# A scheduler priority of 450 instructions for four steps of each slot in a chunked attention kernel

## The chip, the cores and the metric

The kernel runs on one core of one Trainium2 chip. The metric is the device time of one execution in microseconds (us). A core has five engines that each work through their own queue in order: TensorE (PE in the rows, its weight loads PEld), VectorE (DVE), ScalarE (ACT), GpSimd (POOL), and SyncE (SP), which here only issues DMA transfers. They meet through semaphores.

## What is computed

Three layers follow each other: a recurrent attention over 768 steps for 4 batches of 8 heads with 40 dimensions, a layer of 8 experts of which each token uses one, and a dense layer. The part that matters here is the first:

```python
state = np.zeros((B, H, D, D), dtype=np.float32)
for t in range(S):
    y[:, :, t] = np.einsum('bhd,bhde->bhe', rt, state)
    Sa = np.einsum('bhde,bhe->bhd', state, at)
    state_decay = state * wt[:, :, None, :] - np.einsum('bhd,bhe->bhde', Sa, bt)
    state = state_decay + np.einsum('bhd,bhe->bhde', vt, kt)
```

Then `x = _moe_ref(attention output)` and `_moe2_ref(x)`: 3072 tokens of 320 numbers through 1024-wide expert layers and a 2048-wide dense layer.

## The kernel before

The attention works in chunks of 64 steps. Two batches (bb 0 and 1) are taken side by side, and one **slot** is one chunk of one batch with its 8 heads: 12 chunks, 2 batches and 2 pairs of batches give 48 slots, and slots n and n + 2 are the same batch one chunk on. Eight slots (256 steps of two batches) form a **group**; there are six.

Each slot has a **chain** that carries the state from chunk to chunk:

- `stage_a` (L636): eight matmuls `sa` from `vg` and `pw`; ScalarE copies one half of the result into `va`, VectorE multiplies the other half with a mask into `va`.
- `stage_c` (L647): eight matmul pairs `yc` from `va` and `kbr`; VectorE adds the state `sm` and scales it back into `sm`.
- `stage_e` (L663): two transposes `tp` of `sm`, four ScalarE copies into `bds`.
- `stage_r` (L617): ScalarE copies `sm` into `vg`, matmuls `rp` from `bds`, ScalarE copies of `rp` into `vg` and `rs`. With `pw` this `vg` feeds `sa` two slots later.

Beside them stand steps that do not carry the state: `stage_p` (matmuls `pp` from `tt` and `la`, copied into `pw`), `stage_v` (matmuls `rvp`, copied into `vg`, masked by GpSimd into `va`), `stage_d` (output rows `rs`, `yt`) and the router (`xp`, `lg` and small VectorE work).

The rest is **filler**, work for later groups that is written down between the steps of the slots. `prepare` (L429) loads `wz`, `kb` and `ra` and makes two VectorE scans `s` and `q` for a later group; `products` and `sides` make matmuls `lp`, `bp`, `ap` in two PSUM banks, which ScalarE and VectorE empty into `l`, `kbr` and `la`. `inverse` (L516) makes the triangular inverses `tt` of the next group: a VectorE transpose `ul`, 31 pairs `tmp` and `ut` on VectorE, two VectorE transposes `ttc` and `t11`, GpSimd copies into `tt`, then for each half of the group matmuls `zp`, a ScalarE copy `z`, matmuls `yp` and ScalarE copies into `tt`. The `pp` of the next group's first slot needs this `tt`, so the first slot of a group (8, 16, 24, 32, 40) waits for the inverse of its group: the **boundaries** below.

During slot 40 the first expert's weights are loaded (`raw`) and split by ScalarE and VectorE into `we`, six pieces through three buffers. After slot 47 come the experts and the dense layer.

What sets the order: a scheduler takes all instructions of the program and fills each engine's queue. Among those that are ready by its own reckoning it takes the one that was written down first. `run` writes each slot in this order: `stage_a(n)`, `stage_e(n-1)`, filler, `stage_v`, `stage_p` and `stage_r` of slot n+1, `stage_c(n)`, filler, `stage_d(n-1)`, router, loads, filler. The queues are fixed once they are built; at run time each engine takes its next instruction alone and waits for it.

Of the kernel before, what the change touches and what calls it, by code (L numbers as in the profile page):

```python
# [283 lines left out]
class Attention:  # L284
# [330 lines left out]
                                pattern=[[0, 8], [1, C]], compare_op=ALU.is_gt, fill=0.0, base=0, channel_multiplier=-1)  # L615

    def stage_r(self, x):  # L617

        nc = self.nc
        if x.first and x.o.bp:  # L620
            nc.gpsimd.memset(self.sm[:, x.p2], 0.0)
            nc.gpsimd.memset(self.bds[:, x.p4], 0.0)
        for q in range(2):
            nc.scalar.copy(self.by2(x.vg[C:PP, :, q, :D]), self.halves(self.sm[q * HQ:q * HQ + D, x.p2]))
        rp = self.work("rp", [PP, 4, C])
        for i, u in x.prs:
            for r, c in ((slice(0, HQ), slice(0, HQ)), (slice(HQ, P), slice(HQ, PP))):
                nc.tensor.matmul(rp[c, i], lhsT=self.bds[r, u, :c.stop - c.start], rhs=x.r[r, u], start=True, stop=True)  # L628
        for q in range(2):
            nc.scalar.copy(x.vg[C:PP, :, q, D:], rp[q * HQ:q * HQ + D])  # L630
        x.rs = self.p.tile([PP, 4, C], F32, name="rs", bufs=3)
        nc.scalar.copy(x.rs, rp)

    def stage_a(self, x):

        nc = self.nc  # L636
        sa = self.work("sa", [P, 4, VG])
        for i, u in x.prs:
            for q in range(2):
                nc.tensor.matmul(sa[q * 64:q * 64 + 64, i], lhsT=x.pw[:, i, q * C:(q + 1) * C], rhs=x.vg[:, i, q, :], start=True, stop=True)  # L640
        for q in range(2):
            nc.scalar.copy(x.va[C:, :, q, :D], sa[q * 64:q * 64 + 64, :, :D])
        for q in range(2):
            r = slice(q * 64, q * 64 + 64)
            nc.vector.tensor_tensor(x.va[C:, :, q, D:], sa[r, :, D:], self.posmask[r].unsqueeze(1).to_broadcast([C, 4, C]), op=ALU.mult)

    def stage_c(self, x, s0_next):  # L647

        nc = self.nc
        kbr = x.o.kbr[x.half]  # L650
# [10 lines left out]
            nc.vector.tensor_tensor(sm, total, self.by2(s0_next[:, x.p4]).to_broadcast([PP, 2, 2, D]), op=ALU.mult)  # L661

    def stage_e(self, x):  # L663
        nc, k = self.nc, self.k
        tp = self.work("tp", [PP, 2, PP])
        for i in range(2):
# [657 lines left out]
```

## Time and profile before

| | |
|---|---|
| median of 3 runs | 1153.29 us (1152.75 to 1153.3) |
| profiled execution | 1149.13 us, of which the span of the instructions is 1147.3 us |
| slot 0 to slot 47 (first `sa` of each) | 87.3 to 514.1 us |
| experts and dense layer | from about 515 us to the end |
| PE, PEld, DVE, ACT, POOL busy in the span | 89%, 78%, 62%, 50%, 48% |
| PE, DVE, ACT busy between 87.3 and 514.1 us | 379, 322, 322 of 427 us |

Slots are counted by the first `sa` matmul of each. A matmul's record has a modelled end, so a busy PE need not be at its peak; idle time of an engine that nobody waits for costs nothing. In the rows, an arrow names what ended the idle time before an instruction.

### The profile page before, as it was taken

The page shows a single profiled execution, that of the slowest core. Times are in us where ns is not written, and L with a number is a line of the kernel's source. Part 1 is how long each engine was busy: PE and PEld are TensorE (multiplying, and loading weights), DVE is VectorE, ACT ScalarE, POOL GpSimd, SP SyncE. Part 2 cuts the span into 40 slices and gives each one's busy share as a digit, 9 for nine tenths or more (in the row PEclk, how much of TensorE's full clock was granted, in tenths as well). Part 3 has the DMA queues.
Part 4 walks back from the last instruction along what each step waited for, and adds up shares of the span by engine and source line. Part 5 has one row for each costly group of instructions (what it writes and reads, how often), then busy time and mean ns, then how long its engine had stood idle before and what let it go on. Part 6 is the DMA issues. An engine that isn't in the chain of part 4 may idle for free.

```text
span 1147.3 us, 24800 instructions
## 1 busy us (share of the span) xinstructions
PE 1016.7 (89%) x9597; PEld 895.2 (78%) x9597; DVE 715.6 (62%) x1469; ACT 568.4 (50%) x1426; POOL 548.5 (48%) x496
## 2 busy tenths in 40 slices
PE   2649788989899889798898889999999999999997
PEld 2538677867687777687787779999998999999996
DVE  8865887878959869444599984324444545354542
ACT  3637577867787878783554444442222212121211
POOL 6717367555675724233655535452434343434332
PEclk7659899988999999799999989999999999999999
DMA  4613223322322213525688775431000000000000
GB/s 118 203 52 96 63 56 91 89 69 69 94 85 69 56 41 76 137 60 172 179 279 256 242 236 168 131 116 38 24 24 23 23 24 24 23 23 19 29 1 26
DMA packets 98080, 103.35 MB, mean 90 GB/s; under 512 B 58404, under 2 KB 78884, under 8 KB 97956
## 3 DMA queue, kind: packets, MB, share of 16 engines
q1 hardware_dynamic: 95652, 93.83, 28.5%
q0 software_dynamic: 2304, 7.87, 2.1%
q8 instruction: 78, 1.28, 0.5%
q14 instruction: 46, 0.38, 0.1%
HBM read 79.39 MB, written 22.28 MB: 89 GB/s over the span
## 4 chain that ended last, share of the span: by engine, by line
PE 57%; DVE 22%; ACT 6%; issue 5%; DMA 5%; POOL 3%; SPq 0%; DVEq 0%; ACTq 0%; POOLq 0%
PE ph L238 20%; PE po L238 19%; DVE tmp L529 3%; PE lp L483 3%; PE pp L600 2%; DVE ut L531 2%; PE sa L640 2%; PE yc L656 2%; DMA raw<-in_moe_w_dram 2%; DVE s L455 2%; DVE dec L215 2%; DVE dec L218 1%; PE rp L628 1%; DVE q L457 1%; DVE dec L214 1%
## 5 line engine op out<-in xcount | busy, mean ns | idle before, releaser
L229 POOL TENSOR_TENSOR gl<-g,gh 128x512 fp32r<-128x512 f32 x96 | 123.9, 1293 | 211.2 <-ACT gh L228 127.1
L228 ACT ACTIVATE gh<-g 128x512 fp32r<-128x512 f32 x96 | 60.7, 632 | 249.4 <-DVE g L1214 174.5
L1213 DVE TENSOR_SCALAR g<-ph,al 128x512 f32<-128x512 f32 x96 | 72.1, 751 | 156.9 <-POOL gl L229 79.1
L238 PE MATMUL ph<-x2thi,win 128*128 128x512 f32 x480 | 157.0, 392 | 0.0
L238 PE MATMUL po<-wout,gh 128*128 128x320 f32 x768 | 139.1, 309 | 0.0
L238 PEld LDWEIGHTS po<-wout,gh 128*128 128x128 f32 x768 | 122.0, 188 | 5.4
L238 PE MATMUL ph<-x2tlo,win 128*128 128x512 f32 x288 | 113.5, 394 | 0.0
L238 PE MATMUL po<-we,hh 128*128 128x320 f32 (+1 forms) x480 | 91.5, 319 | 19.1 <-DVE hh L1089 13.4
L238 PE MATMUL ph<-xthi,we 128*128 128x448 f32 (+2 forms) x360 | 98.2, 344 | 2.8 <-DVE hl L1089 2.1
L238 PEld LDWEIGHTS ph<-x2thi,win 128*128 128x128 f32 x480 | 88.5, 188 | 13.2
L238 PEld LDWEIGHTS po<-we,hh 128*128 128x128 f32 (+1 forms) x480 | 74.5, 183 | 24.7 <-DVE hh L1089 14.8
L529 DVE TENSOR_TENSOR tmp<-ul,ut 128x31 f32<-128x31 f32 (+15 forms) x186 | 81.4, 437 | 3.7
L238 PE MATMUL po<-wout,gl 128*128 128x320 f32 x384 | 82.9, 311 | 0.0
L614 POOL TENSOR_SCALAR_AFFINE_SELECT va<-vg 64x512 f32<-64x512 f32 x48 | 35.2, 734 | 85.2 <-ACT vg L613 55.8
L238 PE MATMUL ph<-xtlo,we 128*128 128x448 f32 (+2 forms) x216 | 74.1, 344 | 0.3 <-DVE xtlo L271 0.3
L238 PEld LDWEIGHTS ph<-xthi,we 128*128 128x128 f32 x360 | 67.0, 196 | 7.0 <-issue 2.5
L464 POOL TENSOR_TENSOR abd<-ra,q 40x512 f32<-40x512 f32 x44 | 62.4, 1418 | 18.9 <-DVE q L457 5.3
L483 PE MATMUL lp<-kb,abd 128*128 128x128 f32 x352 | 56.4, 307 | 16.7 <-DMA wz<-in_wP_dram 10.7
L1214 DVE SCALAR_TENSOR_TENSOR g<-ph,g 128x512 f32<-128x512 f32 x96 | 66.3, 691 | 3.1
L656 PE MATMUL yc<-va,kbr 128*40 128x104 f32 (+3 forms) x768 | 57.2, 265 | 11.8 <-issue 8.5
L600 PE MATMUL pp<-tt,la 128*104 128x128 f32 x384 | 61.4, 309 | 6.1 <-DVE lg L902 4.1
L677 POOL TENSOR_TENSOR yt<-rs,q 104x256 f32<-104x256 f32 x46 | 34.4, 748 | 67.6 <-DVE rs L676 54.5
(212 smaller groups left out, 2358.0 us busy)
## 6 DMA issues: line engine op xcount, KB each, us to landing
raw<-in_moe_w_dram SPq DMA_DIRECT2D x16, 512.0 KB
rv<-in_rvP_dram SPq DMA_DIRECT2D x48, 160.0 KB
raw<-in_moe_w_dram SPq DMA_DIRECT2D x16, 480.0 KB
kb<-in_kbP_dram SPq DMA_DIRECT2D x44, 160.0 KB
r<-in_moe_w_in_dram SPq DMA_DIRECT2D x10, 512.0 KB
r<-in_moe_w_out_dram SPq DMA_DIRECT2D x10, 512.0 KB
xs_d<-tt SPq DMA_DIRECT2D x8, 560.0 KB
raw<-in_moe_w_dram SPq DMA_DIRECT2D x16, 256.0 KB
```

The lines of the kernel that those rows point to most:

```text
L228: nc.scalar.activation(hi, src, AF.Copy)
L229: return lo_eng.tensor_tensor(lo, src, f32(hi), op=ALU.subtract)
L238: return nc.tensor.matmul(out, lhsT=lhsT, rhs=rhs, start=start, stop=stop)
L464: nc.gpsimd.tensor_tensor(abd[r, :, q * C:(q + 1) * C], ra[r], qc[r, :, :C], op=ALU.mult)
L483: nc.tensor.matmul(lp[:, i], lhsT=abd[:, i, c2, :], rhs=kb[:, i, c2, :], start=True, stop=True)
L529: nc.vector.tensor_tensor(tv, ul[:, j, j + 1:].unsqueeze(2).to_broadcast([P, n, m]), ut[:, j, :m].unsqueeze(1).to_broadcast([P, n, m]), op ...
L600: nc.tensor.matmul(pp[:, i], lhsT=o.la[x.half][:, x.c2, u, :], rhs=o.tt[x.half][:, x.c2, u, :], start=True, stop=True)
L614: nc.gpsimd.affine_select(x.va[:C].rearrange("p a b c -> p (a b) c")[:, :, D:], x.vg[:C].rearrange("p a b c -> p (a b) c")[:, :, D:], patt ...
L656: nc.tensor.matmul(x.yc[r, i, a:], lhsT=kb[:, c], rhs=x.va[:, i, q, a:], start=True, stop=True)
L677: eng.tensor_tensor(yt[:PP, :, x.c2 * C:x.c2 * C + C], x.rs, x.o.q[x.half][:, x.p4, x.c2, :C], op=ALU.mult)
L1213: nc.vector.tensor_scalar(g, ph, 0.0, al[:, f:f + 1], op0=ALU.min, op1=ALU.mult)
L1214: nc.vector.scalar_tensor_tensor(g, ph, 0.0, g, op0=ALU.max, op1=ALU.add)
```

## The change

The bodies of `stage_r`, `stage_a`, `stage_c` and `stage_e` move into `do_r`, `do_a`, `do_c` and `do_e`, and the old names call these inside `high_priority(450)`: to the scheduler their instructions count as if they had been written down 450 instructions earlier. No instruction is added or taken away, `stage_p`, `stage_v`, `stage_d`, the router, the filler and all loads keep their place in the order of writing, and what each instruction depends on is the same.

```diff
     def stage_r(self, x):
+        with self.tc.high_priority(450):
+            self.do_r(x)
+
+    def do_r(self, x):
...
     def stage_a(self, x):
+        with self.tc.high_priority(450):
+            self.do_a(x)
+
+    def do_a(self, x):
...
     def stage_c(self, x, s0_next):
+        with self.tc.high_priority(450):
+            self.do_c(x, s0_next)
+
+    def do_c(self, x, s0_next):
...
     def stage_e(self, x):
+        with self.tc.high_priority(450):
+            self.do_e(x)
+
+    def do_e(self, x):
```

The lines below the first edit shift by 4, 8, 12 and 16; the names stay. The queues up to slot 0, and those of the experts and the dense layer from their first matmuls on, hold the same instructions in nearly the same order.

VectorE around the `va` of slot 8, before (`s`, `q`, `d1q` and `la` are filler, `ul` begins the inverse for slot 16):

```order
L455 SCALAR_TENSOR_TENSOR s<-wz_106,d1s_116 104x520
L491 TENSOR_TENSOR la<-lp,negmask_133 128x4x64
L457 SCALAR_TENSOR_TENSOR q<-wz_105,d1q_119 104x520
L456 RECIPROCAL d1q_119<-s 104x8
L457 SCALAR_TENSOR_TENSOR q<-wz_106,d1q_119 104x520
L645 TENSOR_TENSOR va_402<-sa,posmask_135 64x4x64 x2
L455 SCALAR_TENSOR_TENSOR s<-wz_105,d1s_116 104x520
L491 TENSOR_TENSOR la<-lp,negmask_133 128x4x64
L456 RECIPROCAL d1q_119<-s 104x8
L902 TENSOR_REDUCE lg<-xp 128x8
L522 STREAM_TRANSPOSE ul<-l_1632 128x1024
```

The same place on VectorE now (`va` of slot 8 is L653):

```order
L457 SCALAR_TENSOR_TENSOR q<-wz_106,d1q_119 104x520
L491 TENSOR_TENSOR la<-lp,negmask_133 128x4x64
L455 SCALAR_TENSOR_TENSOR s<-wz_105,d1s_116 104x520
L456 RECIPROCAL d1q_119<-s 104x8
L522 STREAM_TRANSPOSE ul<-l_1632 128x1024
L455 SCALAR_TENSOR_TENSOR s<-wz_106,d1s_116 104x520
L653 TENSOR_TENSOR va_402<-sa,posmask_135 64x4x64 x2
L529 TENSOR_TENSOR tmp<-ul,ut 128x31
```

A `la`, an `s`, the `ul` and a second `s` have moved from behind this `va` to ahead of it.

TensorE at the boundary to slot 40, before and, below, now (`yp` here is the second half of the group's inverse, with buffer numbers):

```order
L557 MATMUL zp_5802<-tt2_126,l1_4975 32x32 x32
L600 MATMUL pp_6259<-tt1_125,la_4977 104x128 x4
...
L565 MATMUL yp_5838<-z1_5835,t11_5719 32x32 x32
L640 MATMUL sa_6297<-vg1_406,pw0_416 64x104 x8
L667 MATMUL tp_6310<-ident_60,sm0_413 104x104 x2
```

```order
L557 MATMUL zp_5802<-tt2_126,l1_4975 32x32 x32
L600 MATMUL pp_6259<-tt1_125,la_4977 104x128
...
L600 MATMUL pp_6259<-tt1_125,la_4977 104x128 x3
L565 MATMUL yp_5838<-z1_5835,t11_5719 32x32 x23
L648 MATMUL sa_6297<-vg1_406,pw0_416 64x104
L683 MATMUL tp_6310<-ident_60,sm0_413 104x104
```

Where the dots stand come the eight `rp` of slot 40: now three of four `pp` follow them, and 9 of the 32 `yp` come behind `sa`.

ScalarE between the last two copies `xr` of slot 40 and the `rp` copies for slot 42, before and now (`we` from `raw_6860` and `raw_6864` are the fifth and sixth weight pieces, `va1` belongs to slot 41, `pw0` to slot 42):

```order
L1039 ACTIVATE we0_6647<-raw_6860 128x960
L901 COPY xr_6363<-xp_6365 128x320
L1039 ACTIVATE we0_6647<-raw_6864 128x640
L901 COPY xr_6364<-xp_6372 128x320
L642 COPY va1_403<-sa_6386 64x4x40 x2
L671 COPY bds0_411<-tp_6399 40x2x40 x4
L613 COPY vg0_404<-rvp_6406 64x4x64 x2
L602 COPY pw0_416<-pp_6418 104x512
```

```order
L917 COPY xr_6364<-xp_6372 128x320
L687 COPY bds0_411<-tp_6399 40x2x40 x4
L1055 ACTIVATE we0_6647<-raw_6860 128x960
L650 COPY va1_403<-sa_6386 64x4x40 x2
L613 COPY vg0_404<-rvp_6406 64x4x64 x2
L1055 ACTIVATE we0_6647<-raw_6864 128x640
L602 COPY pw0_416<-pp_6418 104x512
```

The sixth piece stood ahead of `va` of slot 41 and now stands behind it.

## Rows read from the trace of the kernel before

**Rows 1.** Page, part 1: busy us, share of the span, instructions.

```profile
PE 1016.7 (89%) x9597; PEld 895.2 (78%) x9597; DVE 715.6 (62%) x1469; ACT 568.4 (50%) x1426; POOL 548.5 (48%) x496
```

**Rows 2.** Windows: six groups of slots, the dense layer; columns stand in the first line.

```profile
core 0: us, PE busy (x) PEld busy (x) DVE busy (x) ACT busy (x) POOL busy (x), PEclk, DMA share, GB/s
87.27:179.92 92.65, 81.47 (x1225) 68.22 (x1225) 67.81 (x148) 64.19 (x200) 55.02 (x59) 0.94 0.29 76
179.92:260.79 80.87, 72.30 (x1039) 59.85 (x1039) 63.54 (x159) 59.84 (x190) 49.84 (x53) 0.92 0.31 79
260.79:336.24 75.45, 67.33 (x1020) 56.72 (x1016) 61.59 (x151) 57.73 (x176) 46.91 (x54) 0.91 0.29 77
336.24:411.88 75.64, 67.87 (x1021) 57.41 (x1020) 60.53 (x153) 57.06 (x176) 46.26 (x50) 0.93 0.26 67
411.88:467.61 55.73, 50.35 (x925) 41.91 (x923) 44.73 (x135) 44.62 (x130) 20.00 (x28) 0.97 0.35 88
467.61:514.07 46.46, 40.06 (x565) 33.37 (x561) 23.87 (x70) 38.50 (x107) 12.41 (x17) 0.89 0.31 76
...
770.00:1147.00 377.00, 369.44 (x2118) 335.85 (x2116) 164.19 (x246) 83.61 (x143) 149.62 (x122) 1.00 0.08 23
```

**Rows 3.** Windows, the same columns: slots 7 to 9, around the boundary to slot 8.

```profile
165.00:190.00 25.00, 24.88 (x424) 21.13 (x422) 13.83 (x26) 20.98 (x65) 21.37 (x24) 0.95 0.27 75
```

**Rows 4.** Timeline of VectorE at slot 8: start, us, instruction, shapes, [idle before].

```profile
185.83 0.88 DVE L645 TENSOR_TENSOR va<-sa,posmask 64x256 f32<-64x256 f32 x2
186.74 1.24 DVE L455 TENSOR_TENSOR_SCAN s<-wz,d1s 104x520 f32<-104x520 f32 x1
188.01 0.42 DVE L491 TENSOR_TENSOR la<-lp,negmask 128x256 f32<-128x256 f32 x1
...
189.73 2.00 DVE L522 STREAM_TRANSPOSE ul<-l 128x1024 f32<-128x1024 f32 x1 [0.96 <-POOL l L490]
```

**Rows 5.** Timeline of VectorE: where the inverse begins in two later groups.

```profile
263.34 1.91 DVE L522 STREAM_TRANSPOSE ul<-l 128x1024 f32<-128x1024 f32 x1
...
411.89 1.98 DVE L522 STREAM_TRANSPOSE ul<-l 128x1024 f32<-128x1024 f32 x1 [0.96 <-POOL l L490]
```

**Rows 6.** Timeline of TensorE: filler matmuls ahead of slot 8.

```profile
173.31 1.16 PE L483 MATMUL lp<-kb,abd 128*128 128x128 f32 x8
174.31 0.52 PE L503 MATMUL bp<-ident,kb 104*128 104x104 f32 x4
...
177.37 0.58 PE L507 MATMUL ap<-ident,abd 104*128 104x104 f32 x4
```

**Rows 7.** Timelines of TensorE and ScalarE at the boundary to slot 40.

```profile
465.76 1.92 PE L565 MATMUL yp<-z,t 32*32 32x32 f32 x64
467.61 1.66 PE L640 MATMUL sa<-vg,pw 128*64 128x104 f32 x16
...
465.89 0.76 ACT L630 COPY vg<-rp 40x256 f32<-40x256 f32 x2 [0.48 <-PE rp L628]
```

**Rows 8.** Timeline of ScalarE, slots 40 to 42.

```profile
479.30 1.00 ACT L1039 ACTIVATE we<-raw 128x960 fp32r<-128x960 f32 x1 [0.82 <-DMA raw<-in_moe_w_dram]
...
482.56 0.74 ACT L1039 ACTIVATE we<-raw 128x640 fp32r<-128x640 f32 x1 [1.95 <-DMA raw<-in_moe_w_dram]
...
483.64 0.60 ACT L642 COPY va<-sa 64x160 f32<-64x160 f32 x2
...
486.44 0.58 ACT L602 COPY pw<-pp 104x512 f32<-104x512 f32 x1 [0.47 <-PE pp L600]
```

**Rows 9.** Waits of TensorE, 85 to 515 us: total us, times, longest.

```profile
PE rvp L611 <- DVE lg L902: 5.4, 3, 3.9
```

**Rows 10.** Windows, columns as in rows 2: slots 40 and 41, slots 42 to 46.

```profile
467.61:488.46 20.85, 15.03 (x169) 12.63 (x166) 10.94 (x20) 15.76 (x36) 2.26 (x3) 0.75 0.37 96
488.46:514.07 25.61, 25.03 (x401) 20.73 (x397) 12.93 (x50) 22.74 (x72) 10.14 (x14) 1.00 0.26 60
```

**Rows 11.** Chain of waits near slot 42: start, us, what.

```profile
491.60 0.68 PE rp L628 x15
492.28 0.86 PE yc L656 x15
```

## The prediction

> **What bounds the kernel now.** I read the busy shares of the page first: TensorE 89%, VectorE 62%, ScalarE 50%, GpSimd 48% [rows 1]. They mix stages. The windows part them: in the dense layer TensorE is busy 369 of 377 us, and no instruction of it moves; between slots 0 and 47 (427 us) nobody is full [rows 2]. Per eight slots TensorE is busy 86 to 90%, VectorE 51 to 82%, ScalarE 69 to 83%. What the eye should catch is how uneven the groups are: the second takes 80.87 us, the third 75.45 and the fourth 75.64, for nearly the same busy time on VectorE (63.5, 61.6 and 60.5 us) [rows 2]. The last two groups have less or no filler and run faster.
>
> The time is lost at the boundaries. Around the first `sa` of slot 8, in 25 us, VectorE works 13.8 us and TensorE 24.9 [rows 3]: VectorE has finished the inverse and waits until its copies, `zp`, `yp` and `pp` have gone through the other engines. The next inverse begins (`ul`) at 189.73, 9.8 us after slot 8's first `sa` at 179.92 [rows 2, 4], while in the third and fifth group it begins 2.6 and 0.0 us after [rows 2, 5]. From there to its end VectorE runs nearly without a break, so a late `ul` makes a late boundary to slot 16.
>
> **The change part by part.** No work is added; queues are permuted. I counted filler ahead of each slot's first `sa` in TensorE's two orders: in 27 of 48 slots it is the same. What differs enough to price:
>
> *Slots 8 to 16.* Ahead of slot 8's `va` on VectorE now stand a `la` (0.42 us), a scan `s` (1.24), the `ul` (2.00) and a second `s` (priced like the first): 4.9 us of work [rows 4], put into a stretch where VectorE has 25 - 13.8 = 11.2 us idle [rows 3]. If slot 8 comes no later, the inverse for slot 16 ends up to 4.9 us sooner. The check is the next two groups, which already start their inverse early: they are 5.3 us shorter than the second (80.87 less the mean of 75.45 and 75.64) [rows 2]. I take -5.3; the bounds are 0 and -7.4 (near the end of this inverse about 2.5 us of chain and router work, by the two orders, also falls behind the inverse's last transpose).
>
> *What pays for it.* In slots 4 to 7 the chain now runs ahead of the inverse for slot 8: up to 9 pairs `tmp`, `ut` that stood ahead of a slot's `va` stand behind it. So the inverse ends later in the queue and the filler gathers at the boundary: ahead of slot 8's `sa`, TensorE has 8 `lp`, 4 `bp` and 8 `ap` more and 23 of 64 `yp` less. A group of four `lp` takes 1.16 us (x8 in its row), four `bp` 0.52, four `ap` 0.58 [rows 6], a set of 32 `yp` at most 1.92 [rows 7]: 2.3 + 0.5 + 1.2 - 1.4 = 2.6 us. By its matmul row TensorE is full there (24.88 of 25 us) and would pay all of it; its weight loads fill 21.13 of 25 [rows 3] and leave 3.9 us, so it may pay none. I take +1.5, bounds 0 and +2.6. The Trainium skill (Perfetto Trace Analysis, Identifying the Most-Contended Engine) says that matmul occupancy is a poor measure of headroom, since pipelined matmuls look different in a trace, and that weight-load occupancy should be read instead; by that rule this toll is 0 and the sum below would be -9.8 instead of -8.3, by the matmul row +2.6 and -7.2.
>
> *Boundary to slot 32.* The inverse's first closing transpose `ttc` now precedes slot 30's `va` (0.88 us) and a `la` (0.42) [rows 4]: -1.3, bounds 0 and -2 (yet another slot's small chain work moves behind its second transpose). Slots 16 to 24 keep their VectorE order within a pair or two; I count nothing, the same 61.6 us of work covers it [rows 2].
>
> *Second halves behind `sa`.* At the boundaries to slots 24, 32 and 40, 25, 21 and 9 of the 32 `yp` of the second half now stand behind `sa`. At 40, `sa` starts as these `yp` end (465.76 + 1.92), though its last input copy ended at 466.65 [rows 7]: 1.0 us lost. 55 of 96 `yp` at that price are 3.3 us; at 24 and 32 other filler stays ahead of `sa`, so I take a third, -1.1, bounds 0 and -3.3. The first slot that needs this half comes four slots later, which hides the delay of the `yp` themselves.
>
> *Slots 40 to 42.* Here ScalarE takes the expert's weight pieces in queue order and waits for their loads: 0.82 us for the fifth, 1.95 for the sixth, which ends at 483.30; only then come `va` of slot 41 (483.64) and `pw` of slot 42 (486.44) [rows 8]. TensorE waits behind this too, since VectorE's `lg`, which frees a PSUM bank for `rvp` and `pp`, stood behind the sixth piece: one such wait is 3.9 us [rows 9]. Now `va` stands behind the fifth piece, which ends at 480.30 (3.3 us earlier), `lg` behind the fourth, and `pw` right behind the sixth, at 483.3 (3.1 us earlier). I take -3.1. It may be -1, because VectorE now does slot 40's `yc`, `sm` and `rs` work between the pieces, so the third buffer is freed, and the sixth load begins, later; or -5, because TensorE's clock is granted 0.75 in these slots, after its idle stretch, and 1.00 in the next ones, which take 25.6 us for five slots against 20.9 for two [rows 10].
>
> *Interleaved matmuls.* On TensorE `rp` of one slot and `yc` of the slot before now alternate (four or more changes from one to the other) in 19 slots, before in 5. An `rp` behind a `yc` waits for `va`. Where `yc` has to wait this costs up to a set of `yc`, 0.86 us; where both run back to back, as in the row, it costs nothing [rows 11]. Bounds 0 and 14 x 0.86 = +12; I take +1.0, near the row.
>
> The sum is -5.3 + 1.5 - 1.3 - 1.1 - 3.1 + 1.0 = -8.3 us. Everything behind slot 47 waits for the last slot (its tokens are what the first expert reads) and is triggered from there, so all of it should reach the end. Against the profiled execution, 1147.3 us of span and 1149.1 in all, this gives 1140.8; the median of the runs lies 4.2 us above that execution, and I put the sum there: 1153.3 - 8.3 = 1145.0 us.
>
> **The rivals.** *TensorE is the bound at the boundaries.* Then filler that gathers there costs what is gained in the slots; the gains of the second group and of slot 32 vanish, and of the rest only slots 40 to 42 stay, where TensorE idles: about -2, 1151 us. For it speaks 24.88 of 25 us [rows 3]; against it that the third group does as much in 75.45 us with TensorE at 89% too [rows 2]. *Buffers, not order.* Near it lies that the change hardly does what it says (27 of 48 slots keep their filler): 1153. The Trainium skill (Perfetto Trace Analysis, Optimization Strategy) reads consistent bubbles as a possible lack of SBUF or PSUM for the next tile; a priority would not cure that. The trace agrees for the wait of `rvp` on `lg`, 5.4 us in three waits [rows 9], but these I count under slots 40 to 42.
>
> *More than that.* If TensorE has the room that its weight loads show, the second group gains 7.4 without toll, and the `yp` and slots 40 to 42 reach their far ends: -7.4 - 1.3 - 3.3 - 5 = -17, 1136 us.
>
> *Slower.* Alternating `rp` and `yc` couple two slots: TensorE's queue stops at a `yc` whose `va` is late, and the `rp` behind it, which the next slot's `sa` needs, stops with it. The price is up to 0.86 us [rows 11] in each of 14 more slots, 12 us against gains of 9.3: 1156 us. It decides from 9.3 / 14 = 0.66 us a slot. For it speaks that the scheduler places such pairs by reckoned times; against it that slots with much filler are held by other engines, so that a late `rp` there is partly covered.
>
> **How the numbers follow.** Forecast 1145 (own range 1139 to 1150): 0.46. TensorE bound, 1151: 0.17. Hardly an effect, 1153: 0.06. More, 1136: 0.15. Slower, 1156: 0.16. A measurement of this kernel can tell about 0.2% (2.3 us) from no change, so faster means under 1151.0 and slower over 1155.6: nearly all of the forecast, all of "more" and a third of the TensorE case make 0.66 faster; the rest of that case, the small effect and some of the slower case 0.18 same; 0.16 slower. The range leaves out a tenth at each side: from halfway into "more", 1134, to a little beyond the slower case, 1157.
>
> **What the profile after would show.** Right: slots 8 to 16 near 75 us with `ul` beginning before slot 8's `va`; slot 8's first `sa` between 179 and 183 us; slots 40 and 41 near 17.8 us instead of 20.9, ScalarE's `va` of slot 41 ahead of the sixth piece. Wrong: slot 8 later by 4 us or more (TensorE's toll), slots 17 to 22 and 25 to 29, whose filler did not move, longer than before (the alternation), or an unchanged 80 us for slots 8 to 16.

## The result: 1.0 to 1.3% slower, not 0.7% faster

The changed kernel took 1164.67 us (1158.05 to 1169.29), the kernel before, beside it on the same chip, 1153.02 us: a ratio of 1.010, with an interval from 1.007 to 1.013. Two repeats later gave 1.0125 (1.009 to 1.016) and 1.013 (1.009 to 1.017). The forecast was 1145 us with a range up to 1157; the sign was wrong.

The profiled execution took 1158.05 us, the lowest of the six, with a span of 1156.1 us. The first line of the page answers [rows 1]: TensorE is busy 15.5 us longer, with the same 9597 matmul records.

```profile
PE 1032.2 (89%) x9597; PEld 902.1 (78%) x9597; DVE 714.2 (62%) x1469; ACT 565.9 (49%) x1426; POOL 550.4 (48%) x496
```

The windows of the six groups and of the dense layer, with the columns of [rows 2]:

```profile
87.14:191.04 103.90, 88.73 (x1206) 73.99 (x1205) 74.60 (x156) 67.85 (x215) 65.20 (x68) 0.89 0.29 77
191.04:266.64 75.60, 68.58 (x1045) 56.11 (x1042) 56.18 (x150) 55.78 (x172) 38.80 (x44) 0.93 0.26 68
266.64:344.97 78.33, 72.17 (x978) 59.49 (x978) 62.19 (x151) 57.07 (x178) 48.76 (x54) 0.93 0.30 78
344.97:420.87 75.90, 68.06 (x1026) 55.45 (x1020) 59.11 (x152) 55.13 (x173) 43.82 (x48) 1.00 0.27 67
420.87:479.18 58.31, 54.38 (x960) 44.28 (x955) 45.23 (x136) 45.62 (x133) 21.23 (x30) 0.98 0.24 59
479.18:528.10 48.92, 44.91 (x581) 35.98 (x579) 22.91 (x69) 38.33 (x107) 12.41 (x17) 0.89 0.38 103
...
778.00:1155.00 377.00, 370.44 (x2123) 336.98 (x2123) 164.63 (x247) 84.59 (x146) 151.14 (x123) 1.00 0.08 23
```

Group by group against [rows 2], the change costs 11.3 us in slots 0 to 8, wins 5.3 in slots 8 to 16 (the size that was forecast there), and loses 2.9, 0.3, 2.6 and 2.5 in the others. TensorE's busy time between slots 0 and 47 sums to 396.8 us instead of 379.4; its idle time is 44 us instead of 47. So in this trace the change took 3 us of TensorE's waiting away and added 17 us to its busy time. Of the 14 us that slot 47 is late, 5 come back behind it: from slot 47 to the end it is 628.0 us instead of 633.3. (ScalarE waits for weight loads there in both traces; that this is the reason is not shown.)

With the second and third trace of the changed kernel, and a second of the kernel before, the mean differences by group are +15.3, -5.1, +2.3, +0.8, +3.9, +1.8, and -3.3 from slot 47 on. Most of the loss lies ahead of slot 8; with the group behind it, which wins 5, slots 0 to 16 lose 10 of the 16 us.

**The boundary to slot 8.** Slot 7 comes 3.0 us sooner than before and slot 8 11.2 us later, a step of 29.4 us instead of 15.2. The window answers [rows 3]: TensorE, full before, works 19.1 of 25 us at a granted clock of 0.73.

```profile
165.00:190.00 25.00, 19.07 (x288) 16.30 (x287) 15.98 (x21) 15.08 (x41) 20.84 (x24) 0.73 0.25 71
```

The inverse for slot 8 ends late. From `ul` to `ttc` VectorE had taken 37.7 us with 89 instructions; now it is 43.4 with 105. First the kernel before, then after:

```profile
120.40:158.10 37.70, 29.21 (x399) 24.48 (x392) 35.81 (x89) 21.30 (x64) 12.70 (x13) 0.91 0.18 47
```

```profile
123.80:167.20 43.40, 37.08 (x453) 30.42 (x455) 40.91 (x105) 26.00 (x86) 20.36 (x21) 0.88 0.25 64
```

VectorE (third pair) is nearly full in both; 16 more instructions, the `va` pair of one more slot, two `la` and the router's small ones among them, now stand inside the inverse. `ttc` begins at 167.24 instead of 158.14. Counted from slot 0, slot 8 is 11.4 us later: 3.5 us arise ahead of `ul`, 5.7 between `ul` and `ttc`, 2.1 behind `ttc`.

In the two later traces of the changed kernel the first and the last part are the same within 0.5 us, but the middle is 10.1 and 12.9 us longer than before. VectorE works 7 us more in it, and the rest is idle time, most of it spent waiting for the inputs of `la`, `va` and `yc`, while TensorE's mean clock is lower (0.82 and 0.83). From `ul` to `ttc` in the third trace:

```profile
124.38:175.03 50.65, 40.66 (x454) 33.05 (x456) 43.18 (x106) 26.12 (x87) 20.26 (x21) 0.83 0.20 55
```

Then GpSimd: the router's scatters (L949) now stand ahead of the copies into `tt` (L543), whose first waits 2.66 us for a scatter's landing. Timeline of GpSimd, columns as in [rows 4], and the landing from the chain of waits (start, us, what):

```profile
166.75 1.21 POOL L949 DMA_INDIRECT xs_d<-xr,sli  x1 [0.17 <-DVE ut L531]
168.26 0.98 POOL L949 DMA_INDIRECT xs_d<-xr,sli  x1 [0.30 <-issue]
...
172.59 5.39 POOL L543 TENSOR_SCALAR tt<-ttc 32x512 f32<-32x512 f32 x8 [2.66 <-DMA xs_d<-xr,sli]
```

```profile
168.26 4.14 DMA xs_d<-xr,sli
```

And the filler that now stands ahead of slot 8's `va` on VectorE doesn't just fill idle time; it waits. The second `s` waits for GpSimd's `kb`, and ScalarE's copy of that `s` waits with it; behind this copy stand ScalarE's copies into `bds` and its own half of `va` (timelines of VectorE, against [rows 4], and of ScalarE):

```profile
179.64 1.35 DVE L457 TENSOR_TENSOR_SCAN q<-wz,d1q 104x520 f32<-104x520 f32 x1 [5.24 <-ACT q L424]
...
187.50 1.96 DVE L522 STREAM_TRANSPOSE ul<-l 128x1024 f32<-128x1024 f32 x1 [2.13 <-POOL l L490]
192.62 1.24 DVE L455 TENSOR_TENSOR_SCAN s<-wz,d1s 104x520 f32<-104x520 f32 x1 [3.17 <-POOL kb L460]
195.88 0.88 DVE L653 TENSOR_TENSOR va<-sa,posmask 64x256 f32<-64x256 f32 x2 [2.02 <-ACT va L650]
```

```profile
193.90 0.20 ACT L461 COPY s<-s 104x8 f32<-104x8 f32 x1 [3.77 <-DVE s L455]
```

Even so VectorE's `va` begins 4.8 us after slot 8's first `sa`, before 6.0: what is late is slot 8's `sa`, not the way from it to `va`.

**The middle of a group.** The steps to slots 19, 20, 27 and 28 take 8.1 to 8.7 us instead of 6.0 to 6.1. TensorE in slot 19, first the kernel before, then now:

```profile
290.09 0.68 PE L628 MATMUL rp<-rv,bds 64*64 64x64 f32 x16
290.69 0.93 PE L656 MATMUL yc<-va,kbr 128*64 128x104 f32 x16
291.55 0.58 PE L503 MATMUL bp<-ident,kb 104*128 104x104 f32 x4
```

```profile
297.55 0.33 PE L632 MATMUL rp<-rv,bds 64*64 64x64 f32 x4
297.80 0.39 PE L668 MATMUL yc<-va,kbr 128*64 128x104 f32 x2
298.12 0.33 PE L632 MATMUL rp<-rv,bds 64*64 64x64 f32 x2
...
300.53 0.33 PE L632 MATMUL rp<-rv,bds 64*64 64x64 f32 x4
300.79 0.58 PE L503 MATMUL bp<-ident,kb 104*128 104x104 f32 x4
```

The same 32 matmul records (each matmul leaves two) took 1.46 us, from 290.09 to 291.55, and now fill the 3.24 us from 297.55 to 300.79, with nine changes more from one shape to the other. There is no bracket in these lines: no wait stands in the trace, every piece is simply longer.

### The profile page after: what moved, and what is told of

The parts are those of the page before. It is cut to its first block, busy times and chain, and to the rows that moved or that the text cites. A ratio compares the mean times of both kernels' runs of the same rounds, so it can differ in the third digit from the quotient of the medians.

```text
span 1156.1 us, 24811 instructions
## 1 busy us (share of the span) xinstructions
PE 1032.2 (89%) x9597; PEld 902.1 (78%) x9597; DVE 714.2 (62%) x1469; ACT 565.9 (49%) x1426; POOL 550.4 (48%) x496
## 4 chain that ended last, share of the span: by engine, by line
PE 60%; DVE 19%; DMA 6%; issue 6%; ACT 5%; POOL 3%; SPq 0%; DVEq 0%; POOLq 0%; ACTq 0%
PE ph L238 20%; PE po L238 19%; PE sa L648 3%; PE yc L668 3%; PE pp L600 3%; PE lp L483 3%; DVE tmp L529 3%; DVE s L455 2%; PE rp L632 2%; DVE ut L531 2%; DMA raw<-in_moe_w_dram 2%; PE rvp L611 2%; DVE dec L215 1%; DVE dec L214 1%; DMA kb<-in_kbP_dram 1%
## 5 line engine op out<-in xcount | busy, mean ns | idle before, releaser
L238 PE MATMUL po<-we,hh 128*128 128x320 f32 (+1 forms) x480 | 91.1, 316 | 17.4 <-DVE hh L1105 13.1
L668 PE MATMUL yc<-va,kbr 128*40 128x104 f32 (+3 forms) x768 | 67.9, 264 | 8.6 <-DVE va L653 5.3
L648 PE MATMUL sa<-vg,pw 128*64 128x104 f32 x768 | 61.6, 270 | 13.4 <-ACT pw L602 7.6
L483 PEld LDWEIGHTS lp<-kb,abd 128*128 128x128 f32 x352 | 50.6, 220 | 20.9 <-POOL abd L464 13.6
```

What stands on the lines that cost most here:

```text
L238: return nc.tensor.matmul(out, lhsT=lhsT, rhs=rhs, start=start, stop=stop)
L483: nc.tensor.matmul(lp[:, i], lhsT=abd[:, i, c2, :], rhs=kb[:, i, c2, :], start=True, stop=True)
L668: nc.tensor.matmul(x.yc[r, i, a:], lhsT=kb[:, c], rhs=x.va[:, i, q, a:], start=True, stop=True)
```

## The experiments

Counted in the built order, TensorE goes from `rp` to `yc` or back 69 times between slots 0 and 47 before, and 155 times now. Seven of the runs (e1 to e3 and e11 to e14) came from two chips on which the kernel before took 1164 and 1161 us; their ratios are to that, and microseconds of their traces can be set against the others' only roughly.

**What does a change of shape cost?** Blocks of 80 matmuls of two shapes each, in runs of eight or in pairs:

```diff
+ apart = lambda f, g: [h(i, s) for s in range(10) for h in (f, g) for i in range(4)]
+ mixed = lambda f, g: [h(i, s) for s in range(10) for i in range(4) for h in (f, g)]
```

> Leaves out the whole computation; it only issues matmuls on constant data and writes zeros. It measures the disputed cost by itself: blocks of 80 matmuls of the shape of rp (64 rows, 64 or 40 columns of weights, 64 moving) and 80 of the shape of yc (128 rows, the same weights columns, 104 moving), once in runs of eight (19 changes from one shape to the other), once in pairs (79 changes); the same with rp's shape taken over all 128 rows, so that both use the array alike; the same with the shapes of sa (104 rows, 64 columns) and tp (104 rows, 104 columns). Theory A (a change of shape costs TensorE 0.10 to 0.15 us by itself): 60 more changes make the pairs of rp and yc 6 to 9 us longer than the runs of eight; with 128 rows in both the two orders agree within 1 us; sa and tp pairs are 5 to 9 us longer. Rival B (both orders cost the same back to back, as the prediction had it; the slow stretches of the changed kernel come from waits that the rows do not show): all pairs of blocks agree within 1 us. Rival C (any change of weights or of bank costs, not the use of the array): the blocks with 128 rows in both differ as much as those of rp and yc.

Windows of the six blocks, in the order of the expectation (cut where every 320th record begins; columns: PE, PEld, VectorE, GpSimd, clock):

```profile
103.68:118.31 14.63, 14.63 (x322) 12.64 (x321) 0.00 (x0) 0.00 (x0) 1.00 0.01 2
118.31:141.30 22.99, 22.99 (x322) 15.17 (x322) 0.00 (x0) 0.00 (x0) 1.00 0.01 2
141.30:153.03 11.73, 11.73 (x324) 11.73 (x322) 0.00 (x0) 0.00 (x0) 1.00 0.01 3
153.03:164.83 11.80, 11.80 (x325) 11.80 (x323) 0.00 (x0) 0.00 (x0) 1.00 0.02 4
164.83:189.92 25.09, 25.09 (x327) 22.77 (x322) 0.00 (x0) 0.00 (x0) 1.00 0.01 1
189.92:224.75 34.83, 34.83 (x321) 25.55 (x321) 0.00 (x0) 0.00 (x0) 1.00 0.01 1
```

Sixty more changes cost 8.36 us for `rp` and `yc`, 0.139 us each, and 9.74 us for `sa` and `tp`, 0.162 each. With 128 rows in both shapes they cost nothing (11.73 and 11.80). A second pass over the blocks in the same execution repeats all six times within 0.01 us. Theory A holds, with `sa` and `tp` a little above its 9 us; B and C fall. The weight loads hide it: they grow by 2.5 of the 8.4 us. The Trainium skill (TensorEngine Tiling (Array Packing), Key Properties) says that changing the tiling mode, not just the tile, drains TensorE; the blocks agree, at the two prices above.

**Does the kernel pay that price?** The kernel before, with the order of `rp` and `yc` forced pair by pair, then the same with `rp` over all 128 rows:

```diff
...
+            with (self.tc.issue_after(last.ins) if last else ExitStack()):
+                for r, c in ((slice(0, HQ), slice(0, HQ)), (slice(HQ, P), slice(HQ, PP))):
+                    last = nc.tensor.matmul(rp[c, i], lhsT=self.bds[r, u, :c.stop - c.start], rhs=x.r[r, u], start=True, stop=True)
+            with self.tc.issue_after(last.ins):
...
+                    last = nc.tensor.matmul(y.yc[r, j, a:], lhsT=kb[:, c], rhs=y.va[:, j, q, a:], start=True, stop=True)
```

```diff
-                nc.tensor.matmul(rp[c, i], lhsT=self.bds[r, u, :c.stop - c.start], rhs=x.r[r, u], start=True, stop=True)
+                nc.tensor.matmul(rp[c, i], lhsT=self.bds[:, u, c], rhs=x.r[:, u], start=True, stop=True)
```

> The kernel before, with rp of the next slot and yc of this one forced to alternate pair by pair in every slot: 334 changes between them instead of 69, no priority. Theory A (a change costs 0.139 us of TensorE, and TensorE's time in the slots is mostly on the path): 265 x 0.139 = 37 us more TensorE time, 20 to 37 us of it seen, 1.7 to 3.2% slower. Rival B (TensorE has 47 us of idle time between slots 0 and 47 and takes the changes there): within 8 us of the kernel before, below 0.7%.

> As e7_before_forced_pairs, with rp over all 128 rows, so that the 333 changes cost nothing and only the coupling of two slots is left (rp waits behind a yc whose va is late, and both end later than either alone). Theory A (price of the change): 15 to 35 us below e7_before_forced_pairs, at most 1% above the kernel before. Rival C (the coupling is what costs, up to 0.86 us a slot as the prediction's slower case had it): within 8 us of e7_before_forced_pairs.

Measured: 1.037 (1.032 to 1.043), 1193.6 us, and 1.002 (0.999 to 1.005), 1152.9 us. e7 pays all its 334 changes and e8 none: 40.7 us, 0.122 us a change. Against the kernel before beside them (1150.9 us), e7 has 265 changes more and takes 42.7 us longer, 0.161 us each. Both are somewhat more than theory A had allowed; B and C fall. One set in a slot without waits, TensorE of e7 and of e8:

```profile
302.31 0.33 PE L633 MATMUL rp<-rv,bds 64*64 64x64 f32 x4
302.57 0.39 PE L637 MATMUL yc<-va,kbr 128*64 128x104 f32 x4
...
304.31 0.39 PE L637 MATMUL yc<-va,kbr 128*64 128x104 f32 x4
304.63 0.58 PE L503 MATMUL bp<-ident,kb 104*128 104x104 f32 x4
```

```profile
291.46 0.33 PE L633 MATMUL rp<-rv,bds 128*64 128x64 f32 x4
291.61 0.36 PE L637 MATMUL yc<-va,kbr 128*40 128x104 f32 x4
...
292.48 0.38 PE L637 MATMUL yc<-va,kbr 128*40 128x104 f32 x4
292.79 0.58 PE L503 MATMUL bp<-ident,kb 104*128 104x104 f32 x4
```

2.32 us against 1.33 for a set in the same order: 0.99 us a slot, 0.141 for each of its seven changes. It is the price of the change, not the coupling of two slots: e8 keeps that, and lies within 0.5% of e6 below, which has the same free changes without it.

**Is that what the change lost?** Four ways to take it out: `yc` queued behind the last `rp` (e1), the same with the scatters behind `tt` (e2), no priority for `stage_c` (e3), `rp` over 128 rows in the changed kernel (e4, beside the control c1). The first edit is e1's, around the `yc` matmuls; the second, around the scatters, e2 has besides; the third is e3's; e4 has the edit of e8 above.

```diff
+        with self.tc.issue_after(self.rp_i.ins):
...
+            with self.tc.issue_after(self.tt_i.ins):
...
-        with self.tc.high_priority(450):
-            self.do_c(x, s0_next)
+        self.do_c(x, s0_next)
```

> The changed kernel with one edge more: the yc matmuls of a slot are queued behind the last rp of the next slot, so the two no longer alternate (changes between them on TensorE fall from 155 to 49; before the change there are 69). Theory A (the alternation costs about 0.13 us a change, most of it on the path): 106 changes less, up to 13 us; some of it is covered, so the median falls by 7 to 13 us from 1164.7 to 1152 to 1158; the steps to slots 20 and 28, 8.2 us each in the changed kernel, go back to 6.1 to 6.5; the step from slot 7 to 8 stays near 29 us. Rival B (alternation is free, the loss is the boundary to slot 8 and late weights): 1162 to 1167, the steps to slots 20 and 28 stay above 7.5.

> As e1_rp_first, and the router's two scatters to xs_d are queued on GpSimd behind the last copy into tt that was written down before them (in the changed kernel the first two stand ahead of the tt copies for slot 8, which then wait for the landing of the scatters). Theory A (that wait and what it holds up, kb, yt, ScalarE's check, la, is the late slot 8): the step from slot 7 to slot 8 falls from 29 to 15 to 19 us, and the median is 8 to 13 us below e1_rp_first. Rival B (filler gathered ahead of slot 8 on TensorE and VectorE, the toll of the prediction, is what makes slot 8 late): the step stays above 25 us and the median within 3 us of e1_rp_first.

> One part of the change left out: stage_c has no priority, stage_r, stage_a and stage_e keep theirs. By the built order rp and yc then change 52 times instead of 155, and the first two scatters still stand ahead of the tt copies for slot 8. Theory A (two causes, alternation and scatters; the alternation comes from raising rp and yc together): as e1_rp_first, 1151 to 1158, with 8.2 us steps gone and the step to slot 8 still above 25 us. Rival B (the gains that did come, slots 8 to 16 and the boundary to slot 32, hang on the priority of stage_c): these go too, slots 8 to 16 back at 80 us, and the time stays above 1160.

> The changed kernel once more, as the control of its neighbours on the same chip: the ratio to the kernel before is 1.007 to 1.013 whatever the chip, slot 8 comes 9 to 13 us later than slot 7 does in the kernel before plus its step there, and slot 47 13 to 16 us later. If the loss hung on the chip of the first measurement, the ratio would be below 1.005.

> The changed kernel, but rp reads all 128 rows of rv and takes its weights from a bds with zeros in the other head's block (104 columns wide instead of 64; the router's xr has two buffers instead of three to make room). rp and yc then use the array alike, and by the measurement of m1_shapes a change between them costs nothing. The order on TensorE is nearly that of the changed kernel (154 changes between rp and yc). Theory A (the loss is the price of the changes: 155 at 0.139 us are 21.5 us of TensorE's time, three quarters of it on the path): 10 to 18 us below the changed kernel on the same chip, the steps to slots 19, 20, 27 and 28 back from 8.1 to 8.7 to 6 to 6.5 us. Rival B (the loss is what the order makes engines wait for, at the boundary to slot 8 above all): within 4 us of the changed kernel.

Measured: e1 1.014 (1.010 to 1.018), e2 1.015 (1.011 to 1.020), e3 1.015 (1.011 to 1.020), c1 1.0125, e4 1.0135 (1.010 to 1.017). None gives anything back, and my theory A fell for the changed kernel as a whole. The long steps did shorten (to slots 20 and 28 they take 6.1 and 7.2 us in e1, 6.5 and 6.3 in e4), but others grew. e3's rival B fell as well: without the priority of `stage_c`, slots 8 to 16 still take only 72.0 us. What became of the time is seen in e4, whose order on TensorE is nearly c1's. Windows from slot 0 to 47, first c1, then e4:

```profile
86.28:534.88 448.60, 400.87 (x5776) 330.05 (x5776) 323.24 (x813) 319.84 (x975) 230.68 (x260) 0.92 0.28 73
```

```profile
88.11:525.93 437.82, 377.74 (x5777) 319.90 (x5776) 321.70 (x815) 320.09 (x975) 230.43 (x260) 0.91 0.29 75
```

TensorE is busy 23.1 us less, about what 155 free changes should give, but the stretch is only 10.8 us shorter: idle time rises from 48 to 60 us. (This trace is e4's fastest execution; its median gains 2 us on c1's. The smaller ring `xr` doesn't blur it: ScalarE never waits for a scatter here.) Slot 8 is as late as ever: slots 0 to 8 take 103.8 us in e4 and 104 to 105 in e1, e2 and e3. But in e4 the group behind it takes 70.9 us, so slots 0 to 16 need 174.7 us, before 173.5, and the loss of this trace lies behind slot 16. The scatters are not the cause either: with them behind `tt`, e2 needs 105.2 us to slot 8, e1 without that 105.1. (The wait that e2 takes away is only 1.0 us in e1; from `ttc` to slot 8 e2 takes 20.9 us, e1 22.8, but its `ttc` comes later.)

**Where does the order itself cost?** The change for slots 8 to 47 alone (e5, and e11 without `stage_c`), and for slots 0 to 7 alone (e12, the two sides exchanged; `x.o.start` is true in slots 0 to 7):

```diff
-        with self.tc.high_priority(450):
+        with (ExitStack() if x.o.start else self.tc.high_priority(450)):
```

> One part of the change: the priority holds for slots 8 to 47 alone; slots 0 to 7 are ordered as before. rp and yc change 154 times, the scatters stand behind the tt copies for slot 8 again. Theory A (price of the changes on TensorE, spread over the slots): still 0.5 to 1.1% slower than before, slot 8 at its old place, the loss spread over slots 17 to 31. Rival B (the loss sits in slots 0 to 8, where the chain runs ahead of the inverse on VectorE and pushes it out by 9 us): slot 8 at its old place, 179 to 182, slot 47 not over 4 us later than before, the whole within 0.3% of the kernel before.

> The priority for stage_r, stage_a and stage_e alone, and only from slot 8 on. The queues up to slot 8 are word for word those of the kernel before; rp and yc change 48 times (before 69, changed kernel 155). Theory H (the loss has two parts that stand in for each other, the order in slots 0 to 8 and the price of the changes; each taken away alone left the other): with both gone within 0.4% of the kernel before. Rival I (raising the chain costs in every group by the filler that gathers at its boundary, whatever the changes): still 0.7 to 1.5% slower, and slots 8 to 47 take over 436 us instead of 334.

> The complement: the priority holds for slots 0 to 7 alone. rp and yc change 67 times (before 69). Theory H: slot 8 comes at 189 to 195 (before 179.9), slots 8 to 47 take 328 to 338 us as before, the whole 0.4 to 1.0% slower. Rival I: nearly nothing is lost where only the first group is raised, within 0.3%.

Measured: e5 1.012 (1.009 to 1.016), e11 1.013 (1.008 to 1.017), e12 1.006 (1.003 to 1.008). Windows of slots 0 to 8 and 8 to 47 of e12:

```profile
86.09:197.60 111.51, 94.71 (x1249) 78.98 (x1248) 76.78 (x156) 68.15 (x215) 65.39 (x68) 0.83 0.27 72
197.60:534.74 337.14, 290.82 (x4534) 247.01 (x4529) 244.57 (x658) 254.19 (x760) 163.40 (x193) 0.91 0.28 74
```

Raising slots 0 to 7 is enough for the late slot 8 and half of the loss: in e12 `ttc` begins at 172.6, in e5, where these slots are not raised, at 158.2 as before. Leaving them out doesn't avoid the rest. e5 loses as much as the whole change, so its rival B falls; both of its theories had slot 8 at the old place, and it came 5.9 us later, at the lower clock (below). e11 has no more changes than the kernel before, and its long steps are elsewhere, to slots 16, 24 and 40 (21.1, 17.4 and 23.1 us; in the first kernel, on another chip, 15.2, 11.7 and 13.9). VectorE's wait at the last one (total, times, longest), and the window of that stretch:

```profile
DVE va L653 <- PE yp L565: 17.6, 1, 17.6
```

```profile
481.27:498.82 17.55, 14.41 (x300) 12.08 (x302) 0.00 (x0) 6.61 (x16) 5.08 (x9) 0.50 0.01 2
```

VectorE has nothing to do there from the inverse's last transpose to `va` of slot 40, while the copies into `tt`, `zp`, `yp`, `pp` and `sa` pass through the other engines at the lower clock; `yp` is only the last of them. Yet from `ttc` to slot 40 it is 18.1 us, before 16.2. The group is 13 us longer mainly since its inverse begins late: `ul` comes 10.2 us after slot 32's first `sa`, before 0.0. So H fell for e11 and held for e12 (0.6% and 337.1 us, though slot 8 at 197.6 is past its 195). Rival I fell for e12 and was right for e11 in kind: slots 8 to 47 take 362.4 us, more than the 334 before, though not the 436 that it names. The parts don't add up (1.2 and 0.6% alone, 1.0 to 1.3% together), so they overlap.

**Would the other side deserve the priority?** `prepare`, `products` and `inverse` raised, not the chain:

```diff
+         def soon(fn):
+             with tc.high_priority(450):
+                 fn()
...
+            prep = lambda pg: (lambda: soon(lambda: self.prepare(o, pg)))
...
```

> The kernel before with the same priority of 450 given to the other side: prepare, products, sides and inverse of the next group, not the chain. By the built order rp and yc change 66 times. Theory D (what sets the time of a group is the inverse and what feeds it, the chain has slack inside a group, so the change speeds up the wrong side): the inverse for slot 8 ends no later than before (ttc by 158 us), and the time is 0.3 to 1.0% below the kernel before. Rival E (any order that departs from this one loses at some boundary by filler gathered in front of it): 0.3 to 1.5% slower, with one boundary step of 20 us or more.

Measured 1.004 (1.0005 to 1.007), slot 8 after a step of 29.7 us: theory D falls, E is right. The inverse for slot 8 ended later here too (`ttc` at 165.8).

**128 rows without any priority.** e6 is the kernel before with `rp` over 128 rows; e10 and e13 add the late scatters, e14 is the changed kernel with both.

> The kernel before, without any priority, with rp over 128 rows as in e4_rp_128_rows. Of the 69 changes between rp and yc that it has, 59 are left and cost nothing. Theory A: 69 at 0.139 us are 9.6 us of TensorE's time, so 3 to 9 us faster than before (0.3 to 0.8%). Rival B (TensorE's time is not the limit; waits are): within 0.2%. By this order the first two scatters stand ahead of the tt copies for slot 8, as in the changed kernel: if that is what makes slot 8 late, it is late here too, by 5 us or more.

> e6_before_rp_128_rows with the router's scatters queued behind the tt copies written down before them (in e6 the first two stand ahead of them and slot 8 comes 28 us after slot 7). Theory F (there the scatters' landing on GpSimd, 4.1 us, and the queue behind it are what makes slot 8 late): the step from slot 7 to 8 is 15 to 20 us and the median 5 to 10 us below that of e6, that is 0.6 to 1.1% faster than the kernel before. Rival G (the late slot 8 comes from filler gathered ahead of it and from TensorE's lower clock): the step stays above 24 us, the time within 0.3% of e6.

> e10_before_128_rows_scatter_late, with the room for the wider bds taken from kbr (four buffers instead of five) and the router's three xr buffers kept. In e10 ScalarE waited 12.2 us in 5 waits for the scatters to free xr; those go. Theory J (that wait alone made e10 slow): back to e6 or below, 0.990 to 1.000 of the kernel before. Rival G: the late scatters or the gathered filler themselves cost, above 1.005.

> The changed kernel with both suspects gone: rp over 128 rows (153 changes between rp and yc that cost nothing; kbr has four buffers to make room, xr keeps three) and the scatters behind the tt copies. Theory H: the time is 0.5% slower to 0.5% faster than the kernel before, and the step to slot 8 below 22 us. Rival I (filler gathered at the boundaries): 0.7 to 1.5% slower, the step to slot 8 above 25 us.

Measured: e6 0.998 (0.995 to 1.0003), e10 1.025 (1.020 to 1.030), e13 1.017 (1.012 to 1.022), e14 1.036 (1.031 to 1.040). In e6 slot 8 comes 28.1 us after slot 7, and slots 8 to 47 take 322.4 us instead of 334.2: gain and loss nearly cancel, and it can't be told from the kernel before, nor theory A from B. Note `ttc`: it begins at 165.4 in e6, and between 164.2 and 169.5 in e7, e8, e10 and e13, all without the priority. So a late end of this inverse is not peculiar to the raised chain, and a late slot 8 doesn't decide the total by itself: e6 and e8 make it good in the slots behind. The last three answer another question than I put: my edit holds every pair of scatters behind the newest `tt` written down, in later groups too, and ScalarE then waits for the landing before it can fill `xr` again (e10; total, times, longest):

```profile
ACT xr L901 <- DMA xs_d<-xr,sli: 12.2, 5, 4.3
```

With a third buffer in e13 it was still 8.8 us in 3 waits. They say nothing on slot 8, except that e10 reaches it in 96.7 us and e6, with the scatters in front, in 96.8.

**One program, two clocks.** The last pair repeats both kernels:

> The kernel before once more, for a second trace of it. If the granted clock is what lets two executions of one program differ (as the queues up to slot 8, the same in the kernel before and in e5, suggest: slot 8 at 179.9 and at 185.8), the time from slot 0 to 47 differs from the first trace's 426.8 us by about 0.6 us for each us that TensorE spends more or less at its lower level (61.8 us there), within 5 us. If it differs by more than that at the same clock, something else varies from run to run.

> The changed kernel on the same chip, for a third trace. By the sum that fits the other runs (390 us + 0.57 us for each us at the lower clock + 0.077 us for each change between rp and yc, 155 here), within 6 us from slot 0 to slot 47; the ratio to the kernel before 1.007 to 1.016 again.

Measured: c2 0.999 (0.997 to 1.002), 428.2 us from slot 0 to 47; c3 1.013 (1.009 to 1.017), 449.9 us, where the sum gives 449. For c2 the same sum gives 436, 8 us too much: c2 spends 10 us more at the lower clock and needs only 1.4 us more. Most of it fell into slots 40 to 47, where TensorE idles, so the 0.57 us may be a rate for stretches in which TensorE has work. More telling is e5, whose queues on TensorE, VectorE, ScalarE and GpSimd are the same as before up to the `pp` of slot 8. Windows from slot 7's first `sa` to the `bp` ahead of these `pp`, the kernel before, c2, then e5:

```profile
164.69:174.31 9.62, 9.62 (x204) 8.51 (x204) 3.92 (x14) 7.93 (x24) 8.54 (x12) 0.86 0.12 23
```

```profile
163.36:173.14 9.78, 9.78 (x203) 8.56 (x203) 4.14 (x14) 8.17 (x24) 8.75 (x11) 0.84 0.12 23
```

```profile
164.83:179.64 14.81, 14.81 (x204) 12.95 (x204) 3.89 (x13) 8.62 (x25) 13.10 (x17) 0.50 0.17 47
```

TensorE is busy throughout in all three and does the same matmuls (one record of c2 is missing), but in e5 at the lower of its two levels: 5.2 us more. A set of `lp` takes 2.07 us there, 1.16 at the upper level [rows 6]:

```profile
177.77 2.07 PE L483 MATMUL lp<-kb,abd 128*128 128x128 f32 x8
```

Slot 8 came at 185.8 instead of 179.9, and these 5.2 us are most of it. Whether the chip or the execution makes the difference is not shown.

| run | ratio | changes rp/yc | slots 0-8, us | slots 8-47, us | PE busy, slots | mean clock |
|---|---|---|---|---|---|---|
| before (c2) | 1 | 69 | 92.6 (92.1) | 334.2 (336.0) | 379 (382) | 0.93 (0.92) |
| after (c1, c3) | 1.010 to 1.013 | 155 | 104.0 (107.9, 111.1) | 337.1 (340.7, 338.8) | 397 (401, 405) | 0.93 (0.92, 0.91) |
| e4 | 1.0135 | 154 free | 103.8 | 334.0 | 378 | 0.91 |
| e5 | 1.012 | 154 | 98.5 | 347.2 | 404 | 0.91 |
| e6 | 0.998 | 59 free | 96.8 | 322.4 | 365 | 0.93 |
| e7 | 1.037 | 334 | 103.7 | 361.3 | 421 | 0.90 |
| e8 | 1.002 | 333 free | 98.4 | 330.5 | 370 | 0.92 |
| e9 | 1.004 | 66 | 106.7 | 334.5 | 388 | 0.90 |
| e10 | 1.025 | 55 free | 96.7 | 358.2 | 383 | 0.88 |
| *other chips:* e1 | 1.014 | 49 | 105.1 | 350.8 | 388 | 0.89 |
| e2 | 1.015 | 48 | 105.2 | 350.8 | 387 | 0.89 |
| e3 | 1.015 | 52 | 104.0 | 362.9 | 405 | 0.85 |
| e11 | 1.013 | 48 | 96.8 | 362.4 | 401 | 0.87 |
| e12 | 1.006 | 67 | 111.5 | 337.1 | 386 | 0.89 |
| e13 | 1.017 | 68 free | 98.9 | 358.3 | 384 | 0.87 |
| e14 | 1.036 | 153 free | 107.6 | 369.5 | 403 | 0.85 |

The microseconds are of one profiled execution each, the ratios of medians. A straight line through the traces ahead of c2 and c3 (time at the lower level taken as twice what the mean clock of each group misses to 1, times its length) has the slots' time as 390 us, plus 0.57 us for each us at the lower level, plus 0.077 us for each change that isn't free, with about 4 us of scatter. It goes along with the time and is no proof of a cause: where work comes late TensorE idles, and a lower clock in a stretch with idle time (0.75, with 15.0 of 20.9 us busy) is in the rows of before already [rows 10].

## Why the prediction was wrong, step by step

- **Slots 8 to 16, -5.3:** right in size (-5.1 over the traces) and in sign of it: `ul` begins before slot 8's `va`. But it was conditioned on "if slot 8 comes no later", and that failed, and the size is partly luck: counted from slot 8's first `sa`, `ul` begins 13.4 us sooner in the first trace, not 4.9, while the way from `ul` to `ttc` is 3.1 us longer and that from `ttc` to slot 16 4.9. Nor did VectorE run nearly without a break from this `ul` on: before, it works 48.0 of the 55.4 us to `ttc`.
- **What pays for it, +1.5 with an end at +2.6:** this is the term that broke the forecast. I had seen that up to 9 pairs of the inverse fall behind in slots 4 to 7, and priced only the filler gathered on TensorE, at the upper clock. Not priced was the inverse's own end on VectorE, which the boundary hangs on: 9 to 17 us later in three traces, and slot 8 follows it by 24 us (before 22). On a nearly full VectorE the 5 to 7 us of work let in ahead of that end come out at the boundary, and the waits that this work brings with it come on top. Measured for slots 0 to 8: 11, 15 and 19 us. Whether TensorE's headroom is read from its matmul row (+2.6) or by the rule of the Trainium skill (Perfetto Trace Analysis, Identifying the Most-Contended Engine) from its weight loads (0) was the wrong question: after the change TensorE is busy 19.07 of the 25 us there and its weight loads 16.30, so it is not full by either, and slot 8 waits for the inverse.
- **The interleaved matmuls, +1.0:** wrong was the sentence that they cost nothing where both run back to back. They cost 0.139 us a change by themselves: 86 changes more are 12 us of TensorE's time, and 6 a slot in the 14 slots are 0.85 us, above the 0.66 us from which the slower rival decided. That rival had the size of this term right by a wrong mechanism: not a late `va` (e8), but the change. Only, in the changed kernel it could not be shown to be on the path as a whole: taken out, it came back as idle time and lower clock.
- **Slots 40 to 42, -3.1:** nothing came: 21.7 us instead of 20.9, in the later traces 21.0 and 21.9 against 21.5. `va` of slot 41 did pass the sixth weight piece, but `pw` of slot 41 fell behind the third, which waits for its load; ScalarE and TensorE:

```profile
491.66 1.06 ACT L1039 ACTIVATE we<-raw 128x1024 fp32r<-128x1024 f32 x1 [1.20 <-DMA raw<-in_moe_w_dram]
492.63 0.57 ACT L602 COPY pw<-pp 104x512 f32<-104x512 f32 x1
```

```profile
493.25 0.39 PE L648 MATMUL sa<-vg,pw 128*64 128x104 f32 x2 [1.31 <-ACT pw L602]
```

  The wait moved from slot 42 to slot 41 (14.1 us instead of 8.1, then 7.7 instead of 12.8). I had followed the sixth piece alone past the queue, and not the other five.
- **Boundary to slot 32, -1.3:** that step fell from 18.1 to 13.6 us, more than forecast, while the slots ahead of it lost the same, slots 27 and 28 above all, where the changes stand: 24 to 32 takes 75.9 us as before (75.6). **Second halves behind `sa`, -1.1:** the step to slot 40 is 13.6 to 15.9 us in three traces, before 13.9 and 14.2: no gain.
- **The signs named in advance** did their work: slots 8 to 16 near 75 us (right), slot 8 later by over 4 us (the toll), slots 17 to 22 and 25 to 29 together 3.5 and 3.4 us longer, with all of it in slots 19, 20, 27 and 28 (the alternation).

What stays open: how much of the 15 us ahead of slot 8 is order and how much the lower clock (0.89, 0.86 and 0.85 against 0.94), and why every order with the chain raised from slot 8 on pays 1% or more, whatever else is changed (e1 to e5, e11), while e6, e8 and e9 reach slot 8 late too and stay within 0.4%. The order in slots 0 to 7 is shown as the cause of the late slot 8 (e5 and e12), not as the cause of the whole loss. No experiment held the clock up.

## What to carry to other kernels

A priority for the dependent chain can help only where the chain is what the next stage waits for. Here a group ends with an inverse on a nearly full VectorE, and in the first group the steps let in ahead of its end came out again at the boundary, with their waits on top: find the instruction that the boundary waits for, and count what any reordering puts in front of that one. And when an order on TensorE interleaves two matmul shapes, count the changes between ways of using the array, at 0.12 to 0.16 us each in these runs, before counting waits: no wait shows them.

## What the runs showed of the hardware

- A change between fp32 matmuls over 64 and over 128 rows costs TensorE 0.139 us at the upper clock, between 64 and 104 columns of weights (`sa`, `tp`) 0.162, with no wait in the trace and with little in the weight loads; with the same use of the array it costs nothing (m1). In the whole kernel it was 0.12 to 0.16 us (e7, e8).
- The same 204 matmul records, with TensorE busy throughout, took 9.62 us at a granted clock of 0.86 in one execution and 14.81 us at 0.50 in another: 5.2 us at one boundary, half a per cent of the kernel.
- GpSimd's copies into `tt`, a ring of buffers from one of which earlier transfers to `xs_d` had read, waited for the landing of a scatter to `xs_d` issued just ahead (2.66 us in the changed kernel, 1.0 in e1), though taking that away brought slot 8 no sooner in e2.
